# Accumulator halves and slot sums in four PSUM tiles, combine buffers and the fifth expert in the q region, a twentieth weight place

## The chip, the cores and the metric

The kernel runs on one core of one Trainium2 chip. The metric is the time of one execution on the device in microseconds; the median of three runs is compared. A separate execution was recorded by the hardware profiler, and all times inside the kernel come from it.

## The reference: attention through pooled memory, then a soft mixture of experts

```python
# q, k, v: 8 x 8 heads x 576 x 64; phi: 8 x 8 x 576 x 32; all float32
a = softmax(phi, over the 576 positions)
k_m, v_m = a^T k, a^T v                      # 32 memory slots per head
attn = softmax(q k_m^T / 8) ; out = attn v_m
x = out as 4608 rows x 512

logits = x @ moe_phi                         # 4608 x 32, 32 slots = 8 experts x 4
d = softmax(logits, over the 4608 rows)      # dispatch
slot_input = d^T x                           # 32 x 512
for e in range(8):                           # w1[e]: 512 x 1024, w2[e]: 1024 x 512
    slot_out[e] = relu(slot_input[e] @ w1[e]) @ w2[e]
c = softmax(logits, over the 32 slots)       # combine
return c @ slot_out                          # 4608 x 512
```

The experts' weights are 33.6 MB, half of the 66.65 MB that the kernel reads.

## The kernel before: a planner, an arena and a tail

**Order.** Every step is told to a planner (`add(engine, cost, function, reads, writes)`), which simulates the five engines with estimated costs and issues the steps in the order that comes out. A `Slots` pool is a set of buffers; a `Tile` takes a place of its pool when the planner issues its first step, the place that is free first. Each engine then runs its own queue strictly in that order. A wait between engines is put in wherever two steps touch the same tile; for PSUM, the tensor engine's (TensorE, PE) result memory, two halves of one tile count as the same tile for these waits, as the rows below show.

**Memory.** One large SBUF tensor, `arena` (44288 words per partition), is used twice. First it holds the attention's buffers, stacked from word 0 so that the ones that live longest lie lowest. Later the places for expert weights (`ws`, 2048 words each, 1 MB over the 128 partitions) lie over them, from the top down: 19 places, the lowest at word 5376. Below them lie small buffers of the last stage: `css`, `cxs` (combine), `hss`, `hTs` (hidden layer), `acs` (a copy of the sum over experts). The buffers of the finished output (`ots`) lie over the lowest weight places. A second tensor, the q region (`top`, 4608 words), holds two batches of q, later two weight places (`wqs`), and last the transposed combine weights (`cT`). The pool of `top` is then closed and a pool `late` opened in its place.

**Weights.** SyncE (SP) issues all transfers from one queue, in the planner's order: the inputs of the 8 batches, then 16 loads of w1 (two per expert, `load_w` in `expert_in`) and 16 of w2 (in `expert_out`; the last one in four quarters), then 14 output transfers. A load of a weight waits at the head of that queue until its place is free, and everything behind it waits too. All loads go through L484.

**Expert stage.** When the dispatched slots (`SIM`, L1123) are there, TensorE multiplies them with w1 of each expert (L1215), for the two groups of four experts (`EG`) into one PSUM bank each; `hidden` applies the relu (L1231), transposes (L1240) and copies (L1246). Then it multiplies with w2 (L1266): for each load, four products into columns 0 to 255 (d = 0) and four into columns 256 to 511 (d = 1) of the output row, summed over all experts in `pacc`. The two halves of `pacc` are the two banks of one PSUM tile, `kvbank`.

**Combine.** Between the w2 products, `slots` does four rounds, one for each 1152 rows: softmax of the logits on VectorE (DVE) and ScalarE (ACT) (L1314 to L1336), five transposes on TensorE (L1347), and copies into `cT`. A round's `css` is one buffer, so the next round's L1335 waits for L1347.

**Tail.** `slot_sums`: for d = 0 on VectorE and for d = 1 on ScalarE, half of `pacc` is copied (L1192), and TensorE sums over its four partition groups with a product (L1199) into `so[d]`, the two banks of a second PSUM tile, `scbank`. ScalarE casts `so[d]` to float32r (L1382) and VectorE forms what the cast leaves over (L1387); together they are `sr`. Then come 36 output tiles, `out_mult` (L1396): two products each, evicted by ScalarE or VectorE (L1418, L1420, L1449, L1451) and sent out by SyncE (L1429, L1459). The output tiles go round through the four PSUM tiles `bank0` to `bank3` (named bank_62 to bank_65 in the order below), which `b_m` (first three) and `b_l` (the last) use before.

Of the kernel before, what the change touches and what calls it, by code (L numbers as in the profile page):

```python
# [8 lines left out]
F32 = mybir.dt.float32  # L9
F32R = mybir.dt.float32r  # L10
AF = mybir.ActivationFunctionType
ALU = mybir.AluOpType
# [143 lines left out]
class Slots:  # L156

    def __init__(self, aps, ranges=None, below=(), fifo=False):  # L160
        self.aps = aps
        self.fifo = fifo
# [45 lines left out]
class Tile:  # L208
# [7 lines left out]

    @property
    def ap(self):
        return self.fixed if self.pool is None else self.pool.aps[self.slot]

    def split(self, n):
        self.parts = n
# [13 lines left out]
def act(n, psum=True):  # L236
    return (0.16 if psum else 0.19) + n / 1200.0
# [15 lines left out]
def kernel(  # L253
# [901 lines left out]
    ct_tile = []  # L1155

    def cT_view(i):
        if not ct_tile:
# [3 lines left out]
        return ct_tile[0][:, i * CT_SZ: (i + 1) * CT_SZ]  # L1162

    cTs = Slots(
        [(lambda i=i: cT_view(i)) for i in range(n_ct)], [(TOP, NBP * CT_SZ)] * n_ct, [qs, wqs],
    )


# [9 lines left out]
        load(lambda: t.ap.rearrange("p (a x) -> p a x", a=src.shape[1]), src, 1 << 20, t)  # L1178
        return t

    pacc = b_kv.tile().split(2)
    HD = DM // 2
    accs = acs.tile().split(2)
    sr = keep("sr", [P, 2, DM], dtype=F32R, parts=2)
    so = [Tile(ap=scbank[:, d, :HD]) for d in range(2)]

    def slot_sums():
        for d in range(2):
            x = slice(d * HD, d * HD + HD)
            add(  # L1190
                *((ACT, act(HD)) if d else (DVE, dve(HD))),
                lambda d=d, x=x: (nc.scalar.copy if d else nc.vector.tensor_copy)(  # L1192
                    accs.ap[:, x], pacc.ap[:, d, :HD]
                ),
                r=[pacc.part(d)], w=[accs.part(d)],
            )
            add(
                PE, 0.5,
                lambda d=d, x=x: nc.tensor.matmul(  # L1199
                    so[d].ap, rep.rearrange("p a n -> p (a n)"), accs.ap[:, x],  # L1200
                    start=True, stop=True,
                ),
                r=[accs.part(d), rep_b], w=[so[d]],
            )

    def expert_in(e, hb):
        w1v = w1[e].rearrange("(c p) f -> p c f", p=P)
        w1b = [load_w(w1v[:, 2 * i: 2 * i + 2], wqs if e == E - 1 else ws) for i in range(2)]
        for i in range(2):

            def f(i=i):
                wv = w1b[i].ap.rearrange("p (c f) -> p c f", c=2)
                for c in range(2):
                    for j in range(4):
                        nc.tensor.matmul(  # L1215
                            hb.ap[NS * j: NS * j + NS, :256],
                            SIM.ap[:, 2 * i + c, NS * e: NS * e + NS],
                            wv[:, c, 256 * j: 256 * j + 256],
                            start=(e % EG == 0 and i == 0 and c == 0),
                            stop=(e % EG == EG - 1 and i == 1 and c == 1),  # L1220
                            tile_position=(0, NS * j),
                        )

            add(PE, pe(16, NS, 256, tiles=4), f, r=[SIM, w1b[i]], w=[hb])
# [28 lines left out]
    def expert_out(e):  # L1253
        w2v = w2[e].rearrange("(j p t) d -> p j (t d)", j=4, t=2)
        w2h = w2[e].rearrange("(j p t) d -> p j t d", j=4, t=2)
        for i in range(2):
            last = e == E - 1 and i == 1
            t = ws.tile()
            wide = lambda t=t: t.ap.rearrange("p (j t d) -> p j t d", j=2, t=2)

            def mult(dst, d0, n, start, stop, i=i, wide=wide):
                for t in range(2):
                    for j in range(2):

                        x = 2 * t + j
                        nc.tensor.matmul(  # L1266
                            dst[NS * x: NS * x + NS, :n],
                            hT()[:, 4 * t + 2 * i + j, NS * e: NS * e + NS],
                            wide()[:, j, t, d0: d0 + n],
                            start=start,  # L1270
                            stop=stop,
                            tile_position=(0, NS * x),
                        )

            if not last:
                load(
                    lambda t=t: t.ap.rearrange("p (a x) -> p a x", a=2),
                    w2v[:, 2 * i: 2 * i + 2], 1 << 20, t,
                )
                for d in range(2):  # L1280
                    add(
                        PE, 0.5,
                        lambda d=d, mult=mult, i=i: mult(
                            pacc.ap[:, d], d * HD, HD, e == 0 and i == 0, False
                        ),
                        r=[hTb.part(e // EG), t], w=[pacc.part(d)],
                    )
                continue
            t.split(4)
            for d in range(2):  # L1290
                for j in range(2):
                    load(
                        lambda d=d, j=j: wide()[:, j, :, d * HD: d * HD + HD],
                        w2h[:, 2 * i + j, :, d * HD: d * HD + HD], 1 << 18, t.part(2 * d + j),
                    )
            for d in range(2):
                add(
                    PE, 0.5, lambda d=d, mult=mult: mult(pacc.ap[:, d], d * HD, HD, False, True),
                    r=[hTb.part(e // EG), t.part(2 * d), t.part(2 * d + 1)], w=[pacc.part(d)],
                )  # L1300


# [4 lines left out]
    def slots(bp):  # L1307
# [33 lines left out]
        for t, js in enumerate((range(0, 6, 2), range(6, J, 2))):  # L1341
            tp = b_m.tile()

            def f(js=js, tp=tp):
                for i, j in enumerate(js):
                    n = min(P, (J - j) * HALF)
                    nc.tensor.transpose(  # L1347
                        tp.ap[:n, i * P: i * P + P], csb.ap[:, j * HALF: j * HALF + n], ident
                    )

            add(PE, len(js) * 0.14, f, r=[csb, ident_b], w=[tp], also=[ct])

            def f(js=js, tp=tp, ct=ct):
                x = js[0] // 2 * P
                if js[-1] + 2 <= J:
                    nc.scalar.copy(ct.ap()[:, x: x + len(js) * P], tp.ap[:, : len(js) * P])
                else:
                    y = (len(js) - 1) * P
                    nc.scalar.copy(ct.ap()[:, x: x + y], tp.ap[:, :y])
                    nc.scalar.copy(  # L1360
                        ct.ap()[:HALF, x + y: x + y + P], tp.ap[:HALF, y: y + P]
                    )

            add(ACT, act(len(js) * P) + (0.17 if t else 0.0), f, r=[tp], w=[ct.part(t)])
# [14 lines left out]
    for d in range(2):  # L1379
        x = slice(d * HD, d * HD + HD)  # L1380
        add(
            ACT, act(HD), lambda x=x, d=d: nc.scalar.copy(sr.ap[:, 0, x], so[d].ap),  # L1382
            r=[so[d]], w=[sr.part(d)],
        )
        add(
            DVE, dve(HD),
            lambda x=x, d=d: nc.vector.tensor_tensor(  # L1387
                sr.ap[:, 1, x], so[d].ap, sr.ap[:, 0, x].bitcast(F32), op=ALU.subtract
            ),
            r=[so[d], sr.part(d)], w=[sr.part(d)],  # L1390
        )

    def out_mult(bp, j, po, x):
        y = HALF * (j % 2)
        for t in range(2):
            nc.tensor.matmul(  # L1396
                po.ap[:, : x.stop - x.start],
                cT[bp].ap()[y: y + HALF, j // 2 * P: j // 2 * P + P],
                sr.ap[y: y + HALF, t, x],
                start=(t == 0),  # L1400
                stop=(t == 1),
                tile_position=(y, 0),
            )
# [92 lines left out]
```

## Time and profile before

| | us |
|---|---|
| median of 3 runs | 212.32 (212.27 to 212.84) |
| the profiled execution | 211.16 |
| its span, first to last instruction | 209.4 |
| TensorE busy | 171.1 (82%) |
| VectorE busy | 133.6 (64%) |
| GpSimd busy | 84.4 (40%) |
| ScalarE busy | 69.6 (33%) |
| moved by DMA | 76.47 MB, mean 365 GB/s |

In the views of the profile a row begins with the start and the length in us, then the engine, the source line, the operation and out<-in; x is a count, and a bracket says how long the engine had been idle and who ended that. "SPq" is SyncE's queue issuing a transfer: its length is that of the issue, and the time to landing is told apart. In the chain of waits, "issue" is time in which nothing that the profile shows was waited for. A windows row gives, for a stretch of time, its length, the busy time of TensorE's products, its weight loads, VectorE, ScalarE and GpSimd, the granted clock of TensorE, the busy share of the 16 DMA engines, and GB/s.

### The profile page before, as it was taken

To read this page: it belongs to the slowest core of one execution; us is meant where nothing else is said; L and a number is where in the kernel's file an instruction comes from. 1 tells how busy PE (TensorE), PEld (TensorE's weight loads), DVE (VectorE), ACT (ScalarE), POOL (GpSimd) and SP (SyncE) were. 2 spreads that over 40 slices of the span, in tenths; PEclk is the share of its full clock that TensorE was granted. 3 is DMA by queue.
4 is the path that set the end of the run, shared out by engine and by line. 5 is a ranking of instruction groups with operands and counts; after the bars stand their busy time and mean duration, and the time that the engine had idled before them with its cause. 6 is when DMAs were issued, how large, how long until landed. Compare 5 with 4: busy or idle time off the path is not lost.

```text
span 209.4 us, 5942 instructions
## 1 busy us (share of the span) xinstructions
PE 171.1 (82%) x2571; PEld 109.9 (52%) x2571; DVE 133.6 (64%) x232; ACT 69.6 (33%) x183; POOL 84.4 (40%) x84
## 2 busy tenths in 40 slices
PE   7999777698398997959998979698999998799600
PEld 6677654455265574535655437445555554476300
DVE  7843245969819999987967697467940840278600
ACT  2031426235351644433723344020010330456500
POOL 7199108779780697499971255400000000000000
PEclk9999999969979999999996999999999999969965
DMA  6999999999999999999989999997999998079997
GB/s 206 369 391 391 380 390 380 390 382 386 389 380 393 385 395 408 378 389 392 407 311 408 415 394 394 407 410 250 308 408 412 405 410 286 3 270 414 414 413 295
DMA packets 28986, 76.47 MB, mean 365 GB/s; under 512 B 1824, under 2 KB 6944, under 8 KB 28960
## 3 DMA queue, kind: packets, MB, share of 16 engines
q1 hardware_dynamic: 28960, 76.09, 95.8%
q8 instruction: 20, 0.33, 0.7%
q14 instruction: 6, 0.05, 0.1%
HBM read 66.65 MB, written 9.44 MB: 363 GB/s over the span
## 4 chain that ended last, share of the span: by engine, by line
PE 38%; DMA 22%; DVE 15%; POOL 10%; issue 5%; ACT 2%; SPq 2%; DVEq 1%; POOLq 0%; ACTq 0%
DMA top<-in_q_dram 10%; DMA arena<-in_moe_w_dram 9%; PE kvbank L502 5%; PE bank L811 5%; PE scbank L742 5%; PE bank L1215 5%; PE bank L1396 4%; PE kvbank L625 4%; POOL arena L800 3%; DVE arena L726 3%; DMA out_dram<-arena 3%; POOL arena L588 3%; PE bank L939 2%; POOL arena L777 2%; POOL arena L575 2%
## 5 line engine op out<-in xcount | busy, mean ns | idle before, releaser
L502 PE MATMUL kvbank<-ones 128*128 128x256 f32 x88 | 25.7, 427 | 2.2 <-ACT arena L648 1.1
L575 POOL TENSOR_TENSOR arena<-arena 128x1152 f32<-128x1152 f32 x8 | 21.0, 2629 | 16.0 <-ACT arena L570 13.4
L726 DVE STREAM_TRANSPOSE arena<-top 128x1152 f32<-128x1152 f32 x16 | 21.7, 1361 | 7.3 <-DMA top<-in_q_dram 7.3
L811 PE MATMUL bank<-arena 128*128 128x288 f32 x64 | 21.6, 465 | 4.3 <-DVE arena L803 4.3
L800 POOL TENSOR_TENSOR arena<-arena,ssm 128x576 f32<-128x576 f32 x16 | 18.3, 1152 | 16.1 <-DVE ssm L796 16.1
L588 POOL TENSOR_TENSOR arena<-arena 128x128 f32<-128x128 f32 (+2 forms) x32 | 23.4, 730 | 2.3 <-ACT arena L581 0.3
L742 PE MATMUL scbank<-arena 64*64 64x288 f32 x256 | 21.7, 433 | 3.0 <-DVE arena L756 2.5
L777 POOL TENSOR_TENSOR arena<-arena,smx 128x576 f32<-128x576 f32 x16 | 18.3, 1150 | 11.7 <-DVE smx L772 11.6
L625 PE MATMUL kvbank<-arena 64*32 64x128 f32 x1152 | 20.3, 274 | 1.9 <-issue 1.3
L502 PEld LDWEIGHTS kvbank<-ones 128*128 128x128 f32 x88 | 17.1, 209 | 7.0 <-issue 2.1
L537 DVE TENSOR_REDUCE arena<-arena 128x128 f32<-128x1152 f32 x8 | 17.0, 2137 | 5.5 <-DMA arena<-in_phi_dram 5.5
L625 PEld LDWEIGHTS kvbank<-arena 64*32 64x32 f32 x1152 | 16.3, 106 | 5.9 <-issue 3.8
L756 DVE STREAM_TRANSPOSE arena<-scbank 128x576 f32<-128x576 f32 x16 | 12.3, 766 | 8.8 <-PE scbank L742 8.8
L811 PEld LDWEIGHTS bank<-arena 128*128 128x128 f32 x64 | 11.9, 205 | 10.3 <-DVE arena L803 6.1
L1266 PE MATMUL kvbank<-arena 128*32 128x256 f32 x256 | 16.1, 382 | 1.1 <-DMA arena<-in_moe_w_dram 0.6
L1396 PE MATMUL bank<-sr,cT 64*128 64x512 f32 (+1 forms) x78 | 15.6, 459 | 0.3 <-DVE sr L1387 0.2
L742 PEld LDWEIGHTS scbank<-arena 64*64 64x64 f32 x256 | 9.1, 137 | 10.8 <-DVE arena L756 4.5
L803 DVE STREAM_TRANSPOSE arena<-arena 128x576 f32<-128x576 f32 x16 | 12.1, 758 | 3.8 <-POOL arena L800 3.7
L782 ACT ACTIVATE arena<-arena 128x576 f32<-128x576 f32 x16 | 11.0, 688 | 7.8 <-POOL arena L777 7.8
L1451 DVE COPY arena<-bank 128x512 f32<-128x512 f32 x17 | 11.5, 691 | 3.1 <-PE bank L1396 1.9
L1396 PEld LDWEIGHTS bank<-sr,cT 64*128 64x128 f32 x78 | 10.6, 209 | 5.2 <-DVE arena L1451 3.4
L1215 PE MATMUL bank<-arena,SIM 128*32 128x256 f32 x224 | 12.5, 380 | 0.4 <-DVE SIM L1123 0.4
(128 smaller groups left out, 233.8 us busy)
## 6 DMA issues: line engine op xcount, KB each, us to landing
arena<-in_moe_w_dram SPq DMA_DIRECT2D x29, 1024.0 KB, 11.3
top<-in_q_dram SPq DMA_DIRECT2D x8, 1152.0 KB, 13.8
arena<-in_k_dram SPq DMA_DIRECT2D x8, 1152.0 KB, 11.3
arena<-in_v_dram SPq DMA_DIRECT2D x8, 1152.0 KB, 13.5
out_dram<-arena SPq DMA_DIRECT2D x11, 768.0 KB, 7.1
arena<-in_phi_dram SPq DMA_DIRECT2D x8, 576.0 KB, 8.7
top<-in_moe_w_dram SPq DMA_DIRECT2D x2, 1024.0 KB, 7.3
arena<-in_moe_w_dram SPq DMA_DIRECT2D x4, 256.0 KB, 14.6
```

Source lines behind the costliest of these rows:

```text
L502: lambda: nc.tensor.matmul(warm.ap, ones, ones.unsqueeze(1).to_broadcast([P, 2, P]), start=True, stop=True,),
L537: lambda: nc.vector.tensor_reduce(mx.ap, ph().rearrange("p c j m -> p c m j"), axis=AX.X, op=ALU.max),
L575: lambda: nc.gpsimd.tensor_tensor(ph(), ph(), mb.ap.unsqueeze(2).to_broadcast([P, C, J, M]), op=ALU.subtract),
L588: plus = lambda o, x, y: nc.gpsimd.tensor_tensor(o, x, y, op=ALU.add)
L625: nc.tensor.matmul(acc.ap[M * c: M * c + M, a, : 2 * D], ph()[h0: h0 + HALF, c, j, :], kv()[h0: h0 + HALF, :, c, j * D: j * D + D], start= ...
L726: nc.vector.transpose(qT.ap.rearrange("p (i u y) -> p u i y", i=2, y=Y), qt.ap[:, h * QT_SZ: h * QT_SZ + QT_SZ].rearrange("p (u i x) -> p ...
L742: nc.tensor.matmul(scb.ap[HALF * g: HALF * g + HALF, a, :JY], kb[g].ap[h0: h0 + HALF, i, c].rearrange("p r m -> p (r m)"), qT[g][c // 2].a ...
L777: lambda: nc.gpsimd.tensor_tensor(exv(), exv(), bc(mx), op=ALU.subtract),
L800: lambda: nc.gpsimd.tensor_tensor(exv(), exv(), bc(sm), op=ALU.mult),
L811: nc.tensor.matmul(lp.ap[:, :JY], vpb.ap[:, h, :], aT.ap[:, a * JY: (a + 1) * JY], start=(h == 0), stop=(h == H - 1),)
L1215: nc.tensor.matmul(hb.ap[NS * j: NS * j + NS, :256], SIM.ap[:, 2 * i + c, NS * e: NS * e + NS], wv[:, c, 256 * j: 256 * j + 256], start=(e ...
L1396: nc.tensor.matmul(po.ap[:, : x.stop - x.start], cT[bp].ap()[y: y + HALF, j // 2 * P: j // 2 * P + P], sr.ap[y: y + HALF, t, x], start=(t ...
```

## The change

Four edits go together. `pacc` is no longer one tile of two banks but two tiles, `kvbank` and `scbank`, of which bank 0 is used; `so` moves from the two banks of `scbank` to `bank3` and `bank0`. The buffers `css`, `cxs` and `acs` move from the arena's bottom to a second tensor, `cS`, in the `late` pool on the q region. With that the arena's small buffers shrink from 3936 to 2560 words, and 20 weight places fit, the new one at word 3328. And the two q-region weight places go to w1 of the fifth expert (e = `EG` = 4) instead of the eighth, so that the region is used up earlier.

```diff
-    css, cxs, hss = over([J * HALF], 1), over([JN], 1), over([2 * P], 2)
-    hTs, acs = over([8 * E * (NS + SE)], 1), over([DM], 1)
+    hss = over([2 * P], 2)
+    hTs = over([8 * E * (NS + SE)], 1)
     n_ct = NBP
     NW = (ARENA - small) // W_SZ
     W0 = ARENA - NW * W_SZ
...
+    late_tiles = []
+
+    def late(x, off, n):
+        if not late_tiles:
             top_pool.close()
             pool = ctx.enter_context(tc.tile_pool(name="late", bufs=1, reuse_waits="tile"))
-            ct_tile.append(pool.tile([P, NBP * CT_SZ], F32R, name="cT"))
+            late_tiles.append(pool.tile([P, NBP * CT_SZ], F32R, name="cT"))
+            late_tiles.append(pool.tile([P, J * HALF + JN + DM], F32, name="cS"))
+        return late_tiles[x][:, off: off + n]
+
+    def after_q(x, off, n, count=1):
+        return Slots(
+            [(lambda i=i: late(x, off + i * n, n)) for i in range(count)],
+            [(TOP, CT_ALL)] * count, [qs, wqs], lazy=True,
+        )
+
+    cTs = after_q(0, 0, CT_SZ, n_ct)
+    css, cxs, acs = (
+        after_q(1, 0, J * HALF), after_q(1, J * HALF, JN), after_q(1, J * HALF + JN, DM)
     )
...
-    pacc = b_kv.tile().split(2)
+    pacc = [b_kv.tile(), b_s2.tile()]
...
-    so = [Tile(ap=scbank[:, d, :HD]) for d in range(2)]
+    so = [b_l.tile(), b_m.tile()]
...
-        w1b = [load_w(w1v[:, 2 * i: 2 * i + 2], wqs if e == E - 1 else ws) for i in range(2)]
+        w1b = [load_w(w1v[:, 2 * i: 2 * i + 2], wqs if e == EG else ws) for i in range(2)]
...
-                            pacc.ap[:, d], d * HD, HD, e == 0 and i == 0, False
+                            pacc[d].ap[:, 0], d * HD, HD, e == 0 and i == 0, False
                         ),
-                        r=[hTb.part(e // EG), t], w=[pacc.part(d)],
+                        r=[hTb.part(e // EG), t], w=[pacc[d]],
```

The remaining lines carry the new names through (`pacc[d]`, `so[d].ap[:, :HD]`, `ct.ap` for `ct.ap()`), and `lazy` makes a pool's place be built when it is first used. Lines behind the first edit shift: L484, L1199, L1266 and L1396 of before are L488, L1211, L1278 and L1408 after.

What it moves, engine by engine. First SyncE, the weight loads from the first into the q region (`top`) on. Waits on DMAHW are for an earlier transfer's landing. Before:

```order
L484 DMA top<-in_moe_w_dram 128x2x1024 [waits DMAHW3_49,DMAHW0_49,DVE_49]
L484 DMA arena<-in_moe_w_dram 128x2x1024 [waits PE_49,DMAHW1_49,Activation_49,Pool_49]
L484 DMA arena<-in_moe_w_dram 128x2x1024 [waits DMAHW2_49]
L484 DMA arena<-in_moe_w_dram 128x2x1024
L484 DMA top<-in_moe_w_dram 128x2x1024 [waits DMAHW4_49,DVE_49]
```

After:

```order
L488 DMA top<-in_moe_w_dram 128x2x1024 [waits DMAHW3_49,DMAHW0_49,DVE_49]
L488 DMA arena<-in_moe_w_dram 128x2x1024 [waits PE_49,DMAHW1_49,Activation_49,Pool_49]
L488 DMA arena<-in_moe_w_dram 128x2x1024 [waits DMAHW2_49]
L488 DMA top<-in_moe_w_dram 128x2x1024 [waits DMAHW4_49,DVE_49]
L488 DMA arena<-in_moe_w_dram 128x2x1024
```

The second load into the q region, which waits for VectorE, stands one place earlier, ahead of a load that waits for nothing.

Nine loads on, SyncE comes to the load that takes the last place of the arena that the attention leaves (in both kernels the one that waits for Pool). Before:

```order
L484 DMA arena<-in_moe_w_dram 128x2x1024 [waits DMAHW4_49,DVE_49,PE_49]
L484 DMA arena<-in_moe_w_dram 128x2x1024 [waits DMAHW5_49,PE_49,Pool_49]
L484 DMA arena<-in_moe_w_dram 128x2x1024 [waits DMAHW6_49,PE_49]
L484 DMA arena<-in_moe_w_dram 128x2x1024 [waits DMAHW7_49,PE_49]
L484 DMA arena<-in_moe_w_dram 128x2x1024 [waits DMAHW0_49,PE_49]
```

After:

```order
L488 DMA arena<-in_moe_w_dram 128x2x1024 [waits DMAHW4_49,DVE_49,PE_49]
L488 DMA arena<-in_moe_w_dram 128x2x1024 [waits DMAHW5_49,PE_49,Pool_49]
L488 DMA arena<-in_moe_w_dram 128x2x1024 [waits DMAHW6_49]
L488 DMA arena<-in_moe_w_dram 128x2x1024 [waits DMAHW7_49,PE_49]
L488 DMA arena<-in_moe_w_dram 128x2x1024 [waits DMAHW0_49,PE_49]
```

The load behind it has lost its wait for PE, which was for the first w1 to be used up; that wait now stands one load later.

Last TensorE, from the last load's products to the slot sums. Before:

```order
L1266 MATMUL kvbank<-arena 32x256 [waits DMAHW0_49]
L1266 MATMUL kvbank<-arena 32x256 [waits DMAHW1_49]
L1266 MATMUL kvbank<-arena 32x256 x2
L1266 MATMUL kvbank<-arena 32x256 [waits DMAHW2_49,DVE_49]
L1266 MATMUL kvbank<-arena 32x256 [waits DMAHW3_49]
L1266 MATMUL kvbank<-arena 32x256 x2
L1199 MATMUL scbank<-arena,rep 128x256
L1199 MATMUL scbank<-arena,rep 128x256 [waits Activation_49]
```

After:

```order
L1278 MATMUL kvbank<-arena 32x256 [waits DMAHW0_49]
L1278 MATMUL kvbank<-arena 32x256 [waits DMAHW1_49]
L1278 MATMUL kvbank<-arena 32x256 x2
L1278 MATMUL scbank<-arena 32x256 [waits DMAHW2_49]
L1278 MATMUL scbank<-arena 32x256 [waits DMAHW3_49]
L1278 MATMUL scbank<-arena 32x256 x2
L1211 MATMUL bank_65<-cS,rep 128x256 [waits DVE_49]
L1211 MATMUL bank_62<-cS,rep 128x256 [waits Activation_49]
```

The wait for VectorE (its copy of half 0) has moved from the products of half 1 to the first slot sum. On VectorE and ScalarE the same four steps of the tail stand in the same order; there L1387's first wait is for ScalarE instead of TensorE, and the second L1382 waits for TensorE instead of VectorE. On VectorE the copy L1246 of the first expert group now stands ahead of the first round's L1319, which waits for the q region. TensorE's transposes L1347 stand at the same places among the w2 products as before.

More of the change, by code (lines that the diff above doesn't have):

```diff
@@ L156, with __init__ @@
 class Slots:
-    def __init__(self, aps, ranges=None, below=(), fifo=False):
+    def __init__(self, aps, ranges=None, below=(), fifo=False, lazy=False):
         self.aps = aps
+        self.lazy = lazy
         self.fifo = fifo
@@ L218, in ap @@
     def ap(self):
-        return self.fixed if self.pool is None else self.pool.aps[self.slot]
+        if self.pool is None:
+            return self.fixed
+        x = self.pool.aps[self.slot]
+        return x() if self.pool.lazy else x
     def split(self, n):
@@ L1192, in slot_sums @@
                 lambda d=d, x=x: (nc.scalar.copy if d else nc.vector.tensor_copy)(
-                    accs.ap[:, x], pacc.ap[:, d, :HD]
+                    accs.ap[:, x], pacc[d].ap[:, 0, :HD]
                 ),
-                r=[pacc.part(d)], w=[accs.part(d)],
+                r=[pacc[d]], w=[accs.part(d)],
             )
@@ L1199, in slot_sums @@
                 lambda d=d, x=x: nc.tensor.matmul(
-                    so[d].ap, rep.rearrange("p a n -> p (a n)"), accs.ap[:, x],
+                    so[d].ap[:, :HD], rep.rearrange("p a n -> p (a n)"), accs.ap[:, x],
                     start=True, stop=True,
@@ L1297, in expert_out @@
                 add(
-                    PE, 0.5, lambda d=d, mult=mult: mult(pacc.ap[:, d], d * HD, HD, False, True),
-                    r=[hTb.part(e // EG), t.part(2 * d), t.part(2 * d + 1)], w=[pacc.part(d)],
+                    PE, 0.5, lambda d=d, mult=mult: mult(pacc[d].ap[:, 0], d * HD, HD, False, True),
+                    r=[hTb.part(e // EG), t.part(2 * d), t.part(2 * d + 1)], w=[pacc[d]],
                 )
@@ L1355, in f @@
                 if js[-1] + 2 <= J:
-                    nc.scalar.copy(ct.ap()[:, x: x + len(js) * P], tp.ap[:, : len(js) * P])
+                    nc.scalar.copy(ct.ap[:, x: x + len(js) * P], tp.ap[:, : len(js) * P])
                 else:
                     y = (len(js) - 1) * P
-                    nc.scalar.copy(ct.ap()[:, x: x + y], tp.ap[:, :y])
+                    nc.scalar.copy(ct.ap[:, x: x + y], tp.ap[:, :y])
                     nc.scalar.copy(
-                        ct.ap()[:HALF, x + y: x + y + P], tp.ap[:HALF, y: y + P]
+                        ct.ap[:HALF, x + y: x + y + P], tp.ap[:HALF, y: y + P]
                     )
@@ L1381 @@
         add(
-            ACT, act(HD), lambda x=x, d=d: nc.scalar.copy(sr.ap[:, 0, x], so[d].ap),
+            ACT, act(HD), lambda x=x, d=d: nc.scalar.copy(sr.ap[:, 0, x], so[d].ap[:, :HD]),
             r=[so[d]], w=[sr.part(d)],
@@ L1387 @@
             lambda x=x, d=d: nc.vector.tensor_tensor(
-                sr.ap[:, 1, x], so[d].ap, sr.ap[:, 0, x].bitcast(F32), op=ALU.subtract
+                sr.ap[:, 1, x], so[d].ap[:, :HD], sr.ap[:, 0, x].bitcast(F32), op=ALU.subtract
             ),
@@ L1397, in out_mult @@
                 po.ap[:, : x.stop - x.start],
-                cT[bp].ap()[y: y + HALF, j // 2 * P: j // 2 * P + P],
+                cT[bp].ap[y: y + HALF, j // 2 * P: j // 2 * P + P],
                 sr.ap[y: y + HALF, t, x],
```

6 lines of the change are left out of this document (removed).

## The prediction

> **What bounds the kernel now.** First the page's second part, the span in 40 slices of 5.23 us: only holes in the DMA row can be worth much, because the slices without one run at 380 to 415 GB/s.
>
> ```profile
> DMA  6999999999999999999989999997999998079997
> GB/s 206 369 391 391 380 390 380 390 382 386 389 380 393 385 395 408 378 389 392 407 311 408 415 394 394 407 410 250 308 408 412 405 410 286 3 270 414 414 413 295
> ```
>
> The change touches two holes: slices 27 and 28 (250 and 308 GB/s, 141.3 to 151.8 us), and slices 33 to 35 (286, 3 and 270, 172.8 to 188.4), between the last weight and the first output. The windows view opens the first hole, and SyncE's timeline and landing times (two answers each) say why it is there. The columns that matter in the windows are the last three: granted clock, DMA share, GB/s.
>
> ```profile
> 144.00:145.00 1.00, 0.66 (x4) 0.26 (x2) 0.93 (x6) 0.00 (x0) 0.00 (x0) 1.00 0.78 311
> 145.00:146.00 1.00, 0.94 (x20) 0.60 (x24) 0.56 (x3) 0.00 (x0) 0.00 (x0) 1.00 0.24 74
> 146.00:147.00 1.00, 1.00 (x24) 0.60 (x20) 1.00 (x1) 0.00 (x0) 0.00 (x0) 1.00 0.18 74
> 147.00:148.00 1.00, 1.00 (x24) 0.63 (x20) 1.00 (x2) 0.00 (x0) 0.00 (x0) 1.00 0.90 102
> 148.00:149.00 1.00, 1.00 (x28) 0.57 (x23) 0.93 (x3) 0.29 (x1) 0.00 (x0) 1.00 0.92 356
> ```
> ```profile
> 140.59 0.37 SPq L484 DMA_DIRECT2D arena<-in_moe_w_dram  x1
> ...
> DMA to landing us min/median/max: 8.5/8.5/8.5
> ...
> 146.19 0.37 SPq L484 DMA_DIRECT2D arena<-in_moe_w_dram  x1
> ...
> DMA to landing us min/median/max: 6.8/6.8/6.8
> ...
> 167.92 2.32 SPq L484 DMA_DIRECT2D arena<-in_moe_w_dram  x1
> ...
> DMA to landing us min/median/max: 10.8/10.8/10.8
> ```
>
> At 140.59 SyncE fills the last free weight place; the next load goes out at 146.19, when TensorE has used up the first one. Against 412 GB/s the rows from 144 to 149 lack 101, 338, 338, 310 and 56 KB, 1.14 MB or 2.8 us of traffic. But the share of 0.24 and 0.18 says that about 3 of 16 DMA engines never stopped (0.18 x 16 = 2.9). They are late: the load of 140.59 landed at 149.1, when the others had been idle since about 145, and the load of 146.19 only at 153.0, which is 3.9 us on, though 1 MB takes 2.55 us at 412 GB/s. The last weight lands at 167.92 + 10.8 = 178.7.
>
> The chain of waits shows what hangs on that landing, and TensorE's timeline how near TensorE itself is to the bound.
>
> ```profile
> 157.25 18.82 DMA arena<-in_moe_w_dram
> ...
> 176.12 2.00 PE kvbank L1266 x24
> ...
> 178.14 0.44 DVE arena L1192
> ...
> 178.62 0.78 PE kvbank L1266 x8
> 179.40 0.64 PE scbank L1199 x2
> ...
> 180.07 0.38 ACT sr L1382
> ...
> 180.49 0.71 PE scbank L1199 x2
> ...
> 181.23 0.44 DVE sr L1387
> ...
> 181.69 0.38 ACT sr L1382
> ...
> 182.57 8.07 PE bank L1396 x37
> ```
> ```profile
> 171.42 4.09 PE L1266 MATMUL kvbank<-arena 128*32 128x256 f32 x72
> 176.12 1.97 PE L1266 MATMUL kvbank<-arena 128*32 128x256 f32 x24 [0.61 <-DMA arena<-in_moe_w_dram]
> 178.62 0.78 PE L1266 MATMUL kvbank<-arena 128*32 128x256 f32 x8 [0.54 <-DVE arena L1192]
> 179.33 0.70 PE L1199 MATMUL scbank<-arena,rep 128*128 128x256 f32 x2
> 180.49 0.70 PE L1199 MATMUL scbank<-arena,rep 128*128 128x256 f32 x2 [0.46 <-ACT sr L1382]
> 181.71 2.56 PE L1396 MATMUL bank<-sr,cT 64*128 64x256 f32 x14 [0.20 <-DVE sr L1387]
> ```
>
> So the tail is a strict zigzag between engines, one column half after the other, and its start hangs on the last landing: the last eight products began at 178.62, a moment before it, and the first slot-sum product came at 179.33 = 178.7 + 0.6. TensorE had caught up at 175.5 and stood 0.61 us for a load.
>
> **The change part by part.**
> *Twentieth place.* The load that went out at 146.19 needs no release any more: it follows that of 140.59 at about 141. On the 13 idle engines it fills the hole, up to 2.55 us of the 2.8. On the latest engine it starts when that one is through, at 149.1, and ends 2.55 later, 151.7, or again 3.9 later, 153.0, as in the trace. The load after it ends 2.55 later, at 154.2 to 155.6; now that load, issued second, ends at 153.0 + 2.55 = 155.6. Since all loads after it queue without a pause (up to 18.82 us in the queue), this stays until the end: the last weight lands 0 to 1.3 us earlier if the latest engine rules, 2.5 if no engine were late. I take 0.7, the middle of the first pair, because that late engine is in the rows. The Trainium skill, "DMA: Bandwidth & Descriptors", section "Why a DMA increments its semaphore by 16 and not by 1", has it that the 16 engines of a transfer finish independently and only the full count means landed; by that rule taken strictly the filled hole is worth 0 here, by the mean rate 2.5, and the shares of 0.18 to 0.24 agree with it.
>
> *Can TensorE follow?* 72 of its instructions took 4.09, so the 104 from 171.42 take 5.9 without a wait and end at 177.3. Now the slot sums start at 179.33; TensorE allows 2.0 earlier, not 2.5. At 0.7 earlier the landing still rules: 178.0 + 0.6 = 178.6.
>
> *Four PSUM tiles.* Removed are the wait of the last eight products for VectorE's copy (0.54), that of the second slot-sum product for ScalarE (0.46), and the crossing of VectorE's first and ScalarE's second step. With T the first slot-sum product (now 179.33): today the output products run freely from 181.71 = T + 2.38. After, ScalarE's cast of half 0 starts at T + 0.74 (180.07 - 179.33) and ends at T + 1.12, VectorE's subtraction follows at once to T + 1.6, while TensorE does the second slot sum from T + 0.64 and the first output product behind it; so the run begins at T + 1.65, 0.73 less. Half 1 (cast to T + 1.75, subtraction to T + 2.2) is done before TensorE's six instructions of half 0 (0.86 now, 181.71 to 182.57) end at T + 2.5. The 0.54 is counted inside the landing, not again: without it those products would have waited until 178.7 anyway. Bounds: 0.46 (that wait alone) to 1.2 (both waits and the 0.20).
>
> *Combine buffers and fifth expert in the q region.* The same instructions on the same sizes; what moves is when they may start.
>
> ```profile
> 148.16 0.46 DVE L1319 TENSOR_TENSOR arena<-L,cmx 128x288 f32<-128x288 f32 x1
> 151.11 0.46 DVE L1336 TENSOR_TENSOR arena<-arena 128x288 fp32r<-128x288 f32 x1
> ...
> 153.89 0.28 DVE L1246 COPY arena<-bank 128x128 f32<-128x128 f32 x1
> ...
> 153.33 4.52 PE L1215 MATMUL bank<-arena,SIM 128*32 128x256 f32 x80
> ...
> 161.75 0.77 PE L1347 MATMUL bank<-ident,arena 128*128 128x128 f32 x5
> ```
>
> A round of VectorE takes 3.4 us (148.16 to 151.57) and begins at 148.16. After, it must wait until TensorE is done with the fifth expert, whose second half are the first 16 of the 80 instructions from 153.33: 16 x 56 ns = 0.9, so about 154.6 with the tail of the last. The first round ends at 158.0; TensorE asks for it at 161.75, in an unchanged place. 3.7 us of cover, so 0; if gone, every us over it delays the four rounds. VectorE's hidden-layer copy (L1246), moved ahead of the round, waits until 153.9 and holds up only work that waits longer. Later rounds already wait for the transposes of the one before (single buffer), and keep their times.
>
> *SyncE's order.* The second q-region load moves ahead of an arena load that waited for nothing:
>
> ```profile
> DMA to landing us min/median/max: 8.1/9.2/10.2
> 109.20 0.97 SPq L484 DMA_DIRECT2D arena<-in_moe_w_dram  x2
> ...
> 113.90 0.37 SPq L484 DMA_DIRECT2D top<-in_moe_w_dram  x1
> ```
>
> It still waits for VectorE's transpose until 113.90, and the arena load behind it now goes out at 114.3 instead of 109.7. The load of 109.20 lands 8.1 later, at 117.3, so the engines have 3 us of work left when it goes out: 0. Even a pause there would be made up at 145, where places, not the rate, set the pace.
>
> *Sum.* 0.7 + 0.73 = 1.4. The output stage shifts whole, since its later slices run at 413 to 414 GB/s whatever the moment of its start:
>
> ```profile
> 183.48 2.10 SPq L1429 DMA_DIRECT2D out_dram<-arena  x3
> ```
>
> The profiled execution, 211.16 (span 209.4 and 1.8 around it), would become 209.7. It lies 1.16 below the median of the runs, so from the median: 212.32 - 1.4 = 210.9.
>
> **The rivals.**
> *The late engine rules fully:* 0 instead of 0.7, leaving 0.73: 211.6 (the page named above is on this side). For it: the 3.9 us between the landings at 149.1 and 153.0. Against: 1.3 of that has no reason that must return.
> *No engine is late in the timed executions:* TensorE then bounds, 2.0 + 0.73: 209.6. For it: 13 engines stood still; against: the rows from 145 to 147.
> *The tail isn't shortened* (a wait stays, or the first output product falls behind another): 0.7 alone, 211.6. Against: the order shows those waits gone.
> *The change does nothing,* late engine and an unshortened tail together: 212.3.
> *The other side: the q region comes free late.* If its release came at R, the first transposes (161.75) would slip from R = 158.3 on, the last ones and TensorE's remaining 5.9 us with them. TensorE has 1.3 us to spare over the landing and the tail gains 0.73, so the kernel is slower by over 0.64 us from R = 158.3 + 1.3 + 0.7 + 0.73 + 0.64 = 161.7 on. At R = 163 that is 212.32 + 1.9 = 214.3. For it: VectorE's first write into the region waits for transfers and TensorE both; against: the fifth expert's products end at 154.6, 7 us before that point.
>
> **How the numbers follow.** About 0.3%, 0.64 us, is what a measurement can tell from no change. Forecast 0.45 (own range 210.3 to 211.5); late engine 0.20; no late engine 0.20; tail not shortened 0.06; nothing 0.04; q region late 0.05. Faster: 0.45 + 0.20 and 0.6 of the two cases at 211.6, which lie just past the bound, 0.16: 0.81. Same: the rest of those two, 0.10, and nothing, 0.04: 0.14. Slower: 0.05. The range, 209.2 to 211.9, holds both cases of the late engine, with 0.4 below the case of no late engine for a drained hole larger than I took.
>
> **What the changed profile would show.** Right: two issues within a us at about 141; the windows from 145 to 148 no longer at 74 to 102 GB/s; the last landing near 178.0; in the tail ScalarE's copy of half 1 beside VectorE's of half 0, no DVE wait before the last eight products, and 1.65 us from the first slot sum to the output run; first output DMA near 182.1 (now 183.48). Wrong: a filled hole with the last landing unmoved (late engine), a landing 2 us earlier with TensorE busy up to it, a wait of TensorE before L1347's transposes near 162, or a hole in the DMA at 115.

## The result, and the profile after

The changed kernel takes 209.41 us (median of 4 runs, 208.55 to 210.34) against 212.30 for the kernel before on the same chip. The ratio on record is 0.9887, with a 95% interval of 0.9847 to 0.9926 (the two medians alone give 0.9864, inside that interval). Ratios here and below are to the kernel before on the same chip, without a few runs that the chip disturbed. Three further comparisons, below, gave 0.9868, 0.9898 and 0.9895. That is a gain of 2.2 to 2.9 us, where 1.4 was forecast. The time lies in the range, but at its lower end, and at the figure of the rival "no engine is late" (209.6).

The DMA rows of the page come first, 40 slices of 5.19 us:

```profile
DMA  6999999999999999999988999999999998079996
GB/s 207 367 391 393 381 389 381 390 382 384 390 380 392 387 391 406 345 393 390 378 325 288 400 411 417 405 409 407 400 413 405 412 405 302 2 292 410 417 417 287
```

The hole of 250 and 308 GB/s is gone: from slice 23 to slice 33 no slice is below 400. The one in the tail is still there. (The dip to 325 and 288 near 109 us is the wait for the first load into the q region, ahead of the reordered one; the kernel before has it too, at 106 to 110, and its depth differs by execution.) The windows view for the three microseconds that had 74, 74 and 102 GB/s, then SyncE's timeline for the two loads that now go out together and for the one behind them:

```profile
145.00:146.00 1.00, 0.63 (x2) 0.23 (x2) 0.94 (x5) 0.00 (x0) 0.00 (x0) 1.00 1.03 410
146.00:147.00 1.00, 0.97 (x20) 0.63 (x24) 0.56 (x2) 0.00 (x0) 0.00 (x0) 1.00 1.02 406
147.00:148.00 1.00, 1.00 (x26) 0.57 (x21) 1.00 (x1) 0.00 (x0) 0.00 (x0) 1.00 1.04 414
```
```profile
141.56 0.37 SPq L488 DMA_DIRECT2D arena<-in_moe_w_dram  x1
141.98 0.46 SPq L488 DMA_DIRECT2D arena<-in_moe_w_dram  x1
147.16 0.37 SPq L488 DMA_DIRECT2D arena<-in_moe_w_dram  x1
...
165.95 2.29 SPq L488 DMA_DIRECT2D arena<-in_moe_w_dram  x1
...
DMA to landing us min/median/max: 10.8/10.8/10.8
```

SyncE still stops, from 142.4 to 147.16, but two loads are queued meanwhile and the engines don't run dry. The last weight lands at 165.95 + 10.8 = 176.8, 1.9 earlier than before.

What TensorE waited for is in the view of waits, between its first product behind SIM and the slot sums, first of the kernel before, then of the changed one (us in total, times, longest):

```profile
PE kvbank L1266 <- DMA arena<-in_moe_w_dram: 0.6, 1, 0.6
PE kvbank L1266 <- DVE arena L1192: 0.5, 1, 0.5
```
```profile
PE bank L1227 <- DVE SIM L1127: 0.4, 1, 0.4
```

After that first wait TensorE waits for nothing that this view lists. It has become the bound, as its timeline and the tail behind it show:

```profile
146.03 0.42 PE L1227 MATMUL bank<-arena,SIM 128*32 128x256 f32 x4 [0.40 <-DVE SIM L1127]
...
162.71 0.77 PE L1359 MATMUL bank<-ident,cS 128*128 128x128 f32 x5
...
177.59 0.61 PE L1278 MATMUL scbank<-arena 128*32 128x256 f32 x8
177.84 0.42 DVE L1204 COPY cS<-kvbank 128x256 f32<-128x256 f32 x1 [6.47 <-PE kvbank L1278]
178.27 0.37 ACT L1204 COPY cS<-scbank 128x256 f32<-128x256 f32 x1 [5.20 <-PE scbank L1278]
178.32 1.13 PE L1211 MATMUL bank<-cS,rep 128*128 128x256 f32 x4
179.06 0.80 ACT L1394 CAST sr<-bank 128x256 fp32r<-128x256 f32 x2 [0.41 <-PE bank L1211]
179.46 0.85 DVE L1399 TENSOR_TENSOR sr<-bank,sr 128x256 fp32r<-128x256 f32 x2 [1.20 <-ACT sr L1394]
179.94 2.43 PEld L1408 LDWEIGHTS bank<-sr,cT 64*128 64x128 f32 x19 [0.28 <-DVE sr L1399]
180.91 0.42 DVE L1432 COPY arena<-bank 128x256 f32<-128x256 f32 x1 [0.59 <-PE bank L1408]
181.40 2.47 SPq L1441 DMA_DIRECT2D out_dram<-arena  x3
```

The last eight products (177.59) no longer wait for VectorE's copy of half 0, which now runs beside them; both slot sums stand in one unbroken group at 178.32; the output run starts at 179.94 and the first output transfer goes out at 181.40.

Four moments tell the experiments apart: S, the first product behind SIM; L, the last weight landing (from the trace's landing times); T, the first slot-sum product; O, the first output transfer. Executions differ by up to 2 us in S, for reasons ahead of the change: the transposes of q (L726) that begin at 102.6 in the profile of before begin at 103.6 to 105.1 in the others (at 103.9 and 104.2 where the queue of loads is as before), and the first load whose place in the queue changes goes out only at 109.7. So the distances are compared and not the moments. "To the end" is the span less O.

| profiled execution | S | L-S | T-S | T-L | O-T | to the end |
|---|---|---|---|---|---|---|
| before | 145.06 | 33.66 | 34.27 | 0.61 | 4.15 | 25.9 |
| four PSUM tiles alone | 145.88 | 33.06 | 33.66 | 0.60 | 3.20 | 26.5 |
| changed, nineteen places | 146.99 | 33.14 | 33.75 | 0.61 | 3.20 | 25.8 |
| places alone | 145.63 | 31.12 | 32.86 | 1.74 | 4.15 | 26.2 |
| **changed** | 146.03 | 30.75 | 32.29 | 1.54 | 3.08 | 26.1 |
| changed, again | 146.11 | 31.10 | 32.30 | 1.20 | 3.08 | 25.9 |
| changed, third | 146.77 | 31.79 | 32.40 | 0.61 | 3.19 | 26.6 |
| changed, fourth | 145.59 | 30.97 | 32.29 | 1.32 | 3.08 | 26.5 |
| sums in one tile | 145.93 | 31.92 | 32.87 | 0.95 | 3.20 | 25.8 |
| q region to expert 8 | 146.06 | 31.40 | 32.55 | 1.15 | 3.08 | 26.2 |
| before, 32 products less | 145.50 | 33.38 | 33.98 | 0.60 | 4.15 | 26.7 |
| changed, 32 products less | 145.57 | 31.39 | 32.00 | 0.61 | 3.19 | 26.8 |
| changed, a load less | 146.63 | 28.70 | 32.30 | 3.60 | 3.07 | 26.2 |
| changed, both less | 146.76 | 28.10 | 31.04 | 2.94 | 3.07 | 26.7 |

From S to O the profile of before has 38.42 and that of the changed kernel 35.37, 3.05 less; the spans differ by 1.9 (209.4 and 207.5) because S came 0.97 later in the second execution and the rest took 0.2 longer.

### The profile page after: what moved, and what is told of

The parts are those of the page before. It is cut to its first block, busy times and chain, and to the rows that moved or that the text cites. A ratio compares the mean times of both kernels' runs of the same rounds, so it can differ in the third digit from the quotient of the medians.

```text
span 207.5 us, 5943 instructions
## 1 busy us (share of the span) xinstructions
PE 170.3 (82%) x2571; PEld 109.1 (53%) x2571; DVE 133.3 (64%) x232; ACT 69.8 (34%) x183; POOL 84.4 (41%) x84
## 4 chain that ended last, share of the span: by engine, by line
PE 50%; DVE 16%; DMA 14%; POOL 6%; issue 4%; ACT 2%; SPq 1%; DVEq 1%; POOLq 0%; ACTq 0%
DMA top<-in_q_dram 11%; PE bank L1227 7%; PE bank L815 6%; PE scbank L746 6%; PE kvbank L629 5%; PE kvbank L506 5%; PE kvbank L1278 4%; DMA out_dram<-arena 4%; PE scbank L1278 3%; DVE arena L730 3%; PE bank L1408 3%; PE bank L943 2%; POOL arena L804 2%; DVE arena L760 2%; DVE arena L541 2%
## 5 line engine op out<-in xcount | busy, mean ns | idle before, releaser
L506 PE MATMUL kvbank<-ones 128*128 128x256 f32 x88 | 25.2, 421 | 2.2 <-ACT arena L652 1.1
L629 PE MATMUL kvbank<-arena 64*32 64x128 f32 x1152 | 21.6, 286 | 2.4 <-issue 1.8
L629 PEld LDWEIGHTS kvbank<-arena 64*32 64x32 f32 x1152 | 17.2, 110 | 6.5 <-issue 4.3
L815 PEld LDWEIGHTS bank<-arena 128*128 128x128 f32 x64 | 12.0, 207 | 10.8 <-DVE arena L807 6.4
L1408 PE MATMUL bank<-sr,cT 64*128 64x512 f32 (+1 forms) x78 | 14.2, 420 | 1.4 <-DVE arena L1463 0.8
L1463 DVE COPY arena<-bank 128x512 f32<-128x512 f32 x17 | 11.0, 687 | 3.7 <-DMA out_dram<-arena 2.4
L1408 PEld LDWEIGHTS bank<-sr,cT 64*128 64x128 f32 x78 | 8.3, 184 | 7.3 <-DVE arena L1463 5.3
L776 DVE TENSOR_REDUCE smx<-arena 128x18 f32<-128x576 f32 x16 | 11.8, 738 | 0.3
```

The lines of the kernel that those rows point to most:

```text
L506: lambda: nc.tensor.matmul(warm.ap, ones, ones.unsqueeze(1).to_broadcast([P, 2, P]), start=True, stop=True,),
L629: nc.tensor.matmul(acc.ap[M * c: M * c + M, a, : 2 * D], ph()[h0: h0 + HALF, c, j, :], kv()[h0: h0 + HALF, :, c, j * D: j * D + D], start= ...
L815: nc.tensor.matmul(lp.ap[:, :JY], vpb.ap[:, h, :], aT.ap[:, a * JY: (a + 1) * JY], start=(h == 0), stop=(h == H - 1),)
L1408: nc.tensor.matmul(po.ap[:, : x.stop - x.start], cT[bp].ap[y: y + HALF, j // 2 * P: j // 2 * P + P], sr.ap[y: y + HALF, t, x], start=(t == 0),
```

## The experiments

**The four PSUM tiles alone.** The kernel before, with nothing of the places or the q region.

```diff
-    pacc = b_kv.tile().split(2)
+    pacc = [b_kv.tile(), b_s2.tile()]
...
-    so = [Tile(ap=scbank[:, d, :HD]) for d in range(2)]
+    so = [b_l.tile(), b_m.tile()]
```

> The kernel before with the four PSUM tiles alone (pacc in kvbank and scbank, so in bank3 and bank0); 19 places, combine buffers in the arena, the eighth expert in the q region. Theory (the changed kernel gained some 2 us because the filled hole makes TensorE the bound from SIM on, and some 0.7 to 1 us in the tail): here only the tail, -0.5 to -1.0 us against before, first slot sum still hanging on the last landing (0.6 us after it), first output DMA 3.1 us after the first slot sum instead of 4.15. Rival (the PSUM split carries most of the gain, and the place little): -1.5 us or more. Rival (late engines decide): the last landing varies by 1 to 2 us from the 178.7 of before with the hole unchanged.

Measured: 0.9958 (0.993 to 0.9986), 0.9 us faster. TensorE's timeline of the tail:

```profile
178.32 1.29 PE L1266 MATMUL scbank<-arena 128*32 128x256 f32 x8
179.54 1.25 PE L1199 MATMUL bank<-arena,rep 128*128 128x256 f32 x4
180.72 3.30 PE L1396 MATMUL bank<-sr,cT 64*128 64x256 f32 x20
```

The slot sums start 0.60 after the landing (178.94), as before: the wait that was removed there saves nothing while the landing rules. The gain lies behind T, 4.15 to 3.20.

**The places and the q region alone.** The changed kernel, with the tail put back.

```diff
-    pacc = [b_kv.tile(), b_s2.tile()]
+    pacc = b_kv.tile().split(2)
...
-    so = [b_l.tile(), b_m.tile()]
+    so = [Tile(ap=scbank[:, d, :HD]) for d in range(2)]
```

> The changed kernel with pacc and so back in kvbank and scbank as before; 20 places, combine buffers and the fifth expert in the q region. Theory: the hole at 145 to 148 is filled, TensorE works without a wait for a load from SIM to the last products, but the last eight products wait again for VectorE's copy (0.5 us) and the zigzag of the tail is back: -1.4 to -1.9 us against before. Rival (late engine holds the last landing where it was): -0.3 us or less.

Measured: 0.9954 (0.9914 to 0.9995), 1.0 us faster, less than the 1.4 to 1.9 that had been expected. The chain of waits in the tail shows why it isn't more:

```profile
177.44 0.44 DVE cS L1204
...
177.92 0.64 PE kvbank L1278 x8
178.56 0.64 PE scbank L1211 x2
...
179.65 0.71 PE scbank L1211 x2
```

The last weight landed at 176.75, but the last eight products wait for VectorE until 177.92. In the kernel before those products waited as well, until 178.62, 0.1 before the last landing of 178.72; here nothing covers that wait.

**The changed kernel with nineteen places.**

```diff
-    NW = (ARENA - small) // W_SZ
+    NW = (ARENA - small) // W_SZ - 1
```

> The changed kernel with one weight place less (NW - 1: 19 places, the word range 3328 to 5375 empty); everything else as changed, same order on every engine. Theory: the hole is back, the load behind the last free place waits for the first used-up w1 (5.2 to 5.6 us after the load ahead of it), and the kernel is as e1: -0.5 to -1.0 us against before. Rival (it is the moved buffers or the fifth expert, not the place): as the changed kernel, -2.4 to -2.9 us.

Measured: 0.9977 (0.9954 to 0.9999), 0.5 us faster, at the edge of what was expected. The windows, with the hole back a little later than in the kernel before:

```profile
147.00:148.00 1.00, 1.00 (x20) 0.66 (x24) 0.56 (x2) 0.00 (x0) 0.00 (x0) 1.00 0.77 307
148.00:149.00 1.00, 1.00 (x28) 0.57 (x21) 1.00 (x1) 0.00 (x0) 0.00 (x0) 1.00 0.42 152
149.00:150.00 1.00, 1.00 (x24) 0.60 (x20) 1.00 (x2) 0.00 (x0) 0.00 (x0) 1.00 0.79 82
```

So it is the twentieth place that fills the hole, and neither the combine buffers nor the fifth expert; and with the hole T is again landing + 0.61.

**The changed kernel three times more,** beside the other runs:

> The changed kernel again, beside the three on the same chip. Theory: ratio 0.985 to 0.993, hole filled, TensorE without a wait for a load from SIM on. Late-engine rival: in some executions the last landing comes after TensorE is ready for the last products, and the gain falls to 1.4 us.

> The changed kernel once more, for comparison with the three others on this chip: 0.985 to 0.990 of the kernel before; the last landing 1.2 to 1.5 us ahead of the first slot-sum product.

> The changed kernel once more, for comparison with the three others on this chip: 0.985 to 0.991 of the kernel before.

Measured: 0.9868 (0.9822 to 0.9913), 0.9898 (0.9859 to 0.9936) and 0.9895 (0.9842 to 0.9948). Twice the landing was 1.2 and 1.3 ahead of T; in the third profile it was 0.61 ahead, where 1.2 to 1.5 had been expected, so there the landing ruled once more, and T - S is still 32.40. The two bounds are that close together.

**The two sums in one PSUM tile,** all else as changed. (The slot sums keep their own tiles.)

```diff
-    pacc = [b_kv.tile(), b_s2.tile()]
+    pacc = b_kv.tile().split(2)
```

> The changed kernel with the two slot sums back in one PSUM tile of two banks, so that products of half 1 and the copy of half 0 wait for each other again; twenty places and the rest as changed. Theory (with the hole filled TensorE bounds from SIM to the slot sums, so the wait before the last eight products costs in full): from the first product behind SIM to the first slot-sum product 32.9 us instead of 32.3, from that to the first output DMA about 3.1 as in the changed kernel, 0.5 to 0.6 us slower than it, 0.990 to 0.992 of the kernel before. Rival (the last landing still bounds, the wait hides under it): no difference from the changed kernel, 0.987.

Measured: 0.9904 (0.9882 to 0.9926), beside 0.9898 for the changed kernel on that chip: the times don't resolve it. The profile does, by its waits of TensorE up to T:

```profile
PE kvbank L1278 <- DVE cS L1204: 0.5, 1, 0.5
```

T - S is 32.87, 0.57 more than 32.30, as the theory had it.

**Less work for TensorE, before and after.** Both kernels leave out 16 first-layer products of each of experts 5 and 6; all weights are still loaded.

```diff
-                for c in range(2):
+                for c in range(1 if e in (5, 6) else 2):
```

> The kernel before with the same 32 products left out. Theory (its last landing bounds, set by the hole at 145): within 0.3 us of the kernel before, and the first slot-sum product still 0.6 behind the last landing; a gain of up to 0.5 only if the shorter first-layer work frees the places ahead of the hole sooner. Rival (TensorE bounds the kernel before too): 1.8 us faster.

> The changed kernel without 16 of the first-layer products of each of experts 5 and 6 (their results are left out), 32 instructions and some 1.8 us of TensorE at 56 ns each; every load stays. Theory (TensorE bounds the changed kernel, with the landing 1.2 to 1.5 us ahead of the first slot-sum product, and a product can't follow a landing by less than 0.6): 0.6 to 0.9 us faster than the changed kernel, and then the first slot-sum product comes 0.6 after the last landing, with a load wait of TensorE again. Rival (the landing or VectorE still bounds): no change. Second rival (the weight places come free earlier too, so the landing follows): the whole 1.8.

Measured, of the kernel before: 1.004 (1.0011 to 1.007), nothing gained and a little lost; T is 0.60 behind the landing. Its waits of TensorE show where the 1.8 us went:

```profile
PE kvbank L1266 <- DMA arena<-in_moe_w_dram: 1.8, 2, 1.6
PE kvbank L1266 <- DVE arena L1192: 0.5, 1, 0.5
```

Most of them became waits for the weights: 1.8 instead of the 0.6 of the kernel before. Of the changed kernel: 0.9898 (0.9864 to 0.9933), no gain over the changed kernel beside it (0.9898), where 0.6 to 0.9 us had been expected. TensorE's timeline:

```profile
176.18 0.62 PE L1278 MATMUL scbank<-arena 128*32 128x256 f32 x2
177.00 0.63 PE L1278 MATMUL scbank<-arena 128*32 128x256 f32 x6 [0.20 <-DMA arena<-in_moe_w_dram]
177.57 0.70 PE L1211 MATMUL bank<-cS,rep 128*128 128x256 f32 x2
```

The landing takes over at once, as expected (T - L 0.61), but T - S fell by only 0.3, because L - S was 31.39 in that execution and not 30.75. And the end gave it back: from O on it took 26.8 instead of 26.1 (in the kernel before, 26.7 instead of 25.9). The last section says what the traces show of that.

**A load less, and both less.** To see both bounds at once, expert 5's first-layer products read the first half of its weights twice, and 1 MB isn't loaded; then this and the 32 products less together.

```diff
-        w1b = [load_w(w1v[:, 2 * i: 2 * i + 2], wqs if e == EG else ws) for i in range(2)]
+        n = 1 if e == 5 else 2
+        w1b = [load_w(w1v[:, 2 * i: 2 * i + 2], wqs if e == EG else ws) for i in range(n)]
+        w1b += w1b[: 2 - n]
```

> The changed kernel without one weight load of 1 MB, 2.55 us of traffic (the second half of expert 5's first-layer weights isn't loaded, its products read the first half). TensorE does the same work. Theory (two limits lie within a microsecond: TensorE's work from the first product behind SIM to the slot sums, 32.3, and the last landing plus 0.6): TensorE alone holds the rest, 32.2 to 32.4 from the first product to the first slot-sum product, the last landing 3 to 4 us ahead of that, at most 0.4 us faster than the changed kernel. Rival (the landing alone bounds): 2.5 us faster.

> The changed kernel without that load and without 16 first-layer products of each of experts 5 and 6 (32 instructions, 1.8 us of TensorE). Theory (two limits, so that both have to be moved): 30.4 to 30.8 us from the first product behind SIM to the first slot-sum product instead of 32.3, 1.2 to 1.9 us faster than the changed kernel, where either alone gave at most 0.4. Rival (something else bounds, such as VectorE's combine rounds or the output's start): less than 0.7 faster.

Measured: 0.9845 (0.9794 to 0.9896) and 0.9845 (0.9803 to 0.9886), beside 0.9895 (0.9842 to 0.9948) of the changed kernel on that chip: about 1 us faster both, which these intervals don't tell apart from the changed kernel, nor from each other. The profiles are clear up to O. TensorE's timeline with a load less, then with both less:

```profile
178.20 0.61 PE L1280 MATMUL scbank<-arena 128*32 128x256 f32 x8
178.93 1.13 PE L1211 MATMUL bank<-cS,rep 128*128 128x256 f32 x4
```
```profile
177.06 0.61 PE L1280 MATMUL scbank<-arena 128*32 128x256 f32 x8
177.80 1.13 PE L1211 MATMUL bank<-cS,rep 128*128 128x256 f32 x4
```

With the landing 3.6 ahead of T, T - S stays at 32.30: TensorE alone holds it there. With both less it is 31.04, so 1.26 of the 1.8 come through (30.4 to 30.8 had been expected; the rest holds a new wait of 0.40 for ScalarE's hidden layer, L1245). That the load less alone is 1 us faster in time, which its profile up to O doesn't show, stays open; the execution profiled, 210.0 us, was the slowest of its six (207.2 to 210.0).

**The q region to the eighth expert,** so that the combine buffers come free after all first-layer products.

```diff
-        w1b = [load_w(w1v[:, 2 * i: 2 * i + 2], wqs if e == EG else ws) for i in range(2)]
+        w1b = [load_w(w1v[:, 2 * i: 2 * i + 2], wqs if e == E - 1 else ws) for i in range(2)]
```

> The changed kernel with the q-region places given to the eighth expert instead of the fifth, so that the combine work, whose buffers lie there, may start only after all first-layer products, about 160.4 instead of about 154.6 (first round of VectorE ready about 164, the transposes later among the second-layer products). Theory (the combine work still runs under the second-layer products): within 0.4 us of the changed kernel, 0.986 to 0.991 of the kernel before. Rival (the late region decides, as the prediction's slower case had it): VectorE's last round and the transposes end after the last load, the first slot-sum product is 1 us or more later, 0.992 or more.

Measured: 0.9884 (0.9846 to 0.9922), as the changed kernel. VectorE's first write into the region, TensorE's first transposes, and its last ones:

```profile
160.65 0.46 DVE L1331 TENSOR_TENSOR cS<-L,cmx 128x288 f32<-128x288 f32 x1 [5.92 <-PE bank L1227]
...
164.48 0.76 PE L1359 MATMUL bank<-ident,cS 128*128 128x128 f32 x5
...
174.60 0.74 PE L1359 MATMUL bank<-ident,cS 128*128 128x128 f32 x5 [0.21 <-DVE cS L1348]
```

The region is free 5.2 us later than in the changed kernel (155.44), and it costs a wait of 0.21 at the last transposes; T - S is 32.55. But the planner moved the transposes with it: TensorE's first five stand behind 64 of the w2 products instead of 32, its last five ahead of 56 instead of 104. So the order followed the later release, and a late release under an unchanged order wasn't tested.

## Why the prediction was right, and where its size was off

The forecast's own figure, 210.9, was 1.5 too slow, and the time that came is the one of the rival without a late engine, which had a chance of 0.20. That it fell into the range is owed to the room kept for that rival, and not to the forecast's sum.

**The twentieth place: right in its mechanism, and 0.7 was too small.** Both issues came within half a microsecond, the windows are at 406 to 414 GB/s, and the last landing moved by more than the 0.7 that was taken: L - S is 33.1 to 33.7 in four profiles with the hole, and 30.8 to 31.9 in eight with it filled and every weight loaded, 2.0 less on average. The step that failed is "I take 0.7 ... because that late engine is in the rows". Those rows were one execution. The trace records a landing once for each of the 16 engines. There they finished the load of 140.59 between 145.1 and 149.1; the same load in the three other profiles with the hole had them spread over 1.5, 2.0 and 1.8 us (145.99 to 147.47, 147.72 to 149.69, 146.05 to 147.89). With 4.0 that execution was the extreme of four.

What made that engine late stays open. It was late long before the hole: in the profile of before the last of the 16 was 1.7 us behind the first on the load of 119.58 (landed 128.1), 3.1 on that of 124.72 (132.3) and 4.8 on that of 125.19 (136.5), and the gap stayed above 4.5 up to the load ahead of the hole (142.0 to 146.6). One packet of 4 KB took 1.17 us at 128.5, where most take 0.16, but the record doesn't name its engine. In the window from 147.0 to 149.2 the DMA view shows one packet of another queue, the instruction queue:

```profile
q8 instruction: 1, 0.02, 5.6%
```

It is 16 KB, and lasted from 147.1 to 149.1, up to the moment of that late landing. But it came after the lateness and added none to this load, which landed 2.4 us behind the one ahead of it (146.64 to 149.07), no more than 1 MB takes (2.55). The Trainium skill's page "DMA: Bandwidth & Descriptors", section "Why a DMA increments its semaphore by 16 and not by 1", has it that the engines finish independently, and those spreads agree. The 0 for the filled hole was the prediction's own reading of that rule, and the measurement decides against it; its own figure for the latest engine, 151.7 instead of 153.0, was 1.3 earlier already.

**TensorE's cap: right, and it became the bound.** "TensorE allows 2.0 earlier": T - S went from 34.27 to 32.29, by 1.98, and stays at 32.30 when the landing is moved away altogether. Against the typical nineteen-place kernel with the four tiles (33.7) the gain in T is 1.4. What the prediction called a sign of its being wrong, "a landing 2 us earlier with TensorE busy up to it", is what came.

**The tail: right in its mechanism, 1.07 instead of 0.73** (0.95 where the landing still sets T, as with the four tiles alone). The output run begins at T + 1.62 (179.94 - 178.32), as worked out (1.65). Two terms were too small. Half 0's first six instructions were priced at 0.86, from 181.71 to 182.57, but that stretch held a wait of 0.28 for VectorE's subtraction of half 1 (L1387); without it VectorE's first copy into the output comes at T + 2.59, and O at T + 3.08. And "the 0.54 is counted inside the landing, not again" holds only while the landing rules: with the hole filled, sums in one tile cost 0.57 in T - S. So the two halves of the change are worth more together, by about that much: alone 0.9 and 1.0 us in time, together 2.2 to 2.9.

**The q region: right.** Its first write was put at 154.6, 9.54 behind S; the profile after:

```profile
155.44 0.46 DVE L1331 TENSOR_TENSOR cS<-L,cmx 128x288 f32<-128x288 f32 x1 [0.74 <-PE bank L1227]
```

That is 9.41 behind S. TensorE's first transposes stand at S + 16.68 (162.71), before at S + 16.69. The slower rival put the point from which a late region decides at 161.7; the experiment with the eighth expert went to 160.65 - 1.00 = 159.65 in that profile's time (its S is 1.00 later) and lost 0.25 in T, with transposes that the planner had moved back. By the prediction's own sum that release would make TensorE's transposes some 1.3 late in an unchanged order (159.65 against 158.3), and a TensorE that is the bound has nothing to spare. What kept the rival away in the changed kernel is the 3.7 us of cover that the prediction worked out (3.8 by the profile), and not the 7 us, which count in spare time that TensorE no longer has.

**SyncE's order: right.** The windows of 2 us at the place named show no hole:

```profile
114.00:116.00 2.00, 2.00 (x8) 1.34 (x7) 1.18 (x2) 0.46 (x1) 0.74 (x1) 0.51 1.00 391
116.00:118.00 2.00, 2.00 (x17) 0.92 (x16) 0.00 (x0) 0.40 (x2) 0.41 (x1) 0.64 1.02 416
```

**The shift of the output stage: nearly.** "Shifts whole" left out that it takes 25.8 to 26.8 from the first issue on, by execution.

## What to carry to other kernels

A pause in a queue that is filled moves the bound to the next limit, so work out that limit before summing the gains; here TensorE stood 2.0 us behind, and the forecast had that number but didn't bet on it. When two limits end within a microsecond of each other, a wait that was covered by the one costs in full under the other: price each edit with the other edits made, and test by relieving each limit alone and both together. And before a rate or a lag is taken from one execution, look whether the same rows would come again in a second one; that of the late engine didn't.

## What the runs showed of the hardware

The end of the output can hang on one late DMA engine, and, as the times suggest, on where an instruction fetch falls. In every profile a 16 KB packet of the instruction queue begins between 182 and 185 us, about when the output does, except in the three kernels with 32 products (64 instructions of TensorE) less: there it begins at 190 to 193. In the changed kernel with 32 products less, the DMA view of 190.0 to 191.1 has it:

```profile
q8 instruction: 1, 0.02, 5.3%
```

Of the 16 engines one then finishes the output transfer of 185.80 at 193.7, the other fifteen by 191.8, and it stays behind: at the last transfer it is 1.4 us later than the others (206.5 and 205.1). The two other kernels of the three end in the same way, 1.3 and 1.4 us, and all three need 26.7 to 26.8 us from O to the end. In the changed kernel the packet runs from 182.1 to 183.5, and one engine finishes the first output transfer at 184.9, the others by 183.5; at the end it is level with them, and the output took 26.1. That the fetch made the engine late is argued from the times, as the record doesn't name the packet's engine. Nor is it the whole account: in the fourth profile of the changed kernel, with the packet at 182.6, one engine stays 1.2 us behind to the end (26.5), and in the third the end took 26.6 with all engines level. The Trainium skill, "Runtime: NRT & Kernel Launch", section "Instruction fetch mechanics", tells of such blocks of 16 KiB, fetched by the sequencer through a DMA queue of its own, and calls the cost of crossing one mostly hidden; beside a queue of transfers that sets the end, one engine of 16 was 1.5 and 1.9 us late in these two profiles. Whether a kernel whose fetch falls into the idle stretch between 177 and 181 would end sooner wasn't tried.

Also, a pause of the DMA queue lines its engines up again, but not for long. With the hole, the load behind it landed on all 16 within 0.9 to 1.1 us in three of four profiles, 2.3 in the fourth, where the load two places ahead had a spread of 1.9 to 4.6; in the eight profiles without the hole and with every weight loaded the same load has 1.5 to 3.3. By the last weight the spread is 1.6 to 2.1 with the hole and 1.6 to 2.8 without. So of the 2.55 us of a load that is moved into the pause, the first of the 16 engines ends the last weight 2.3 us earlier behind S, on average, and the last engine, which is the landing, 2.0.
